# Fp32 value products in one query half of a clustered attention kernel with a maxout layer

## The chip, the cores and the metric

The kernel runs on one NeuronCore of one Trainium2 chip. Its engines are TensorE (PE in the rows, with PEld for its weight loads), VectorE (DVE), ScalarE (ACT), GpSimd (POOL) and SyncE (SP, which issues the DMAs). The metric is the device time of one execution in microseconds; 706.71 us is the median of three runs of the kernel before.

## The reference

```python
def _attn_ref(q, k, v, centroids):            # q, k, v: (4, 8, 768, 64)
    scale = 1.0 / np.sqrt(D)
    ...                                        # q_n, k_n, c_n: rows divided by their norm
    q_assign = np.argmax(np.einsum('bhsd,hcd->bhsc', q_n, c_n), axis=-1)    # 16 clusters
    k_assign = np.argmax(np.einsum('bhsd,hcd->bhsc', k_n, c_n), axis=-1)
    mask = q_assign[:, :, :, None] == k_assign[:, :, None, :]
    scores = scale * np.matmul(q, k.transpose(0, 1, 3, 2))
    scores = np.where(mask, scores, -1000000000.0)
    scores = scores - np.max(scores, axis=-1, keepdims=True)
    attn = np.exp(scores)
    attn = attn / (np.sum(attn, axis=-1, keepdims=True) + 1e-09)
    return np.matmul(attn, v).astype(np.float32)

def _moe_ref(x, w1, w2, w3, w_out):           # x: (3072, 512), w1..w3: (512, 768), w_out: (768, 512)
    h = np.maximum(np.maximum(x @ w1, x @ w2), x @ w3)
    return (h @ w_out).astype(np.float32)
```

All inputs and the output are fp32. The heads of the attention's output are joined to x.

## The kernel before

Most products are done in fp16 as sums of three: a tile is split into a high half (its fp16 value) and a low half (the rest, in fp16 again), and high x high, high x low and low x high are added in PSUM.

The attention goes by batch (4), query half (2, `gi`, three tiles of 128 queries each) and head pair (4): 32 visits (`visit`). A visit has 6 tiles (`tile_units`), one for each of two heads and three query tiles; a tile's number, counted over the whole program, is its `step` (0 to 191). One tile is 128 queries by 768 keys:

- `pe`: 4 matmuls make the scores in a PSUM tile `big` (L1252, L1254). Query and key carry mask rows.
- `mx`: VectorE scales them and takes the row minimum of their negative (L1263, and a small read of the accumulator).
- `exp`: ScalarE makes the exponentials and their row sums (L1269), into an SBUF tile `e` or in place in PSUM.
- Then the weights are turned, so that keys lie on the partitions, and split in two halves in the tile `pt`. Steps in `BY_PE` (even steps below 40): TensorE turns the fp32 tile with 6 transposes into another `big` (`ptr`, L1300), one copy makes the high half (`scaled`, L374 on ScalarE, L378 on VectorE) and VectorE subtracts for the low half (L1308). Other steps: the high half (L374, L376, L378) and the low half (L1275, in batches 1 to 3 also L1328) are made in SBUF in the tile `hl`, and one DMA transpose writes `pt` (L1278).

When a visit's 6 tiles are done, `av` adds 36 matmuls of 384 columns into one `big` (L1203). In batch 0 the row sums are spread over the partitions by 6 small fp32 products (`sums`, L1195), copied (`spread`) and multiplied in (`mult`, L1222), and the result is split in halves into `x16`. `ffn` then takes a half of a batch (384 tokens): 18 units of 12 matmuls (`hid`, L1409, weights `w16a` and `w16b`), whose maxima are taken by VectorE (L1423), and three units `outp` (L1464). It needs all four visits of its half.

Ahead of this the program prepares q and k per head pair (`prep`, with cluster products L778 and L787), v (`v_first` for batch 0, which loads v, takes its largest value with L917, scales and splits it; `v_prep` for the others), and the expert weights (`weights`). The tiles have fixed numbers of places (`caps`): 3 `big` in PSUM, 2 `e`, 4 `hl`, 4 `stage`.

The program is a list of units. `ORDER` gives the order in which they are written to the engines' queues, `HANDS` the engine (V, S, G, Q) of each unit that has a choice. Each engine works through its own queue in that order.

Of the kernel before, what the change touches and what calls it, by code (L numbers as in the profile page):

```python
# [27 lines left out]
0 3 1 4 2 5 7-14 6 16 15 18 19 51 52 173 151 30 54 21 17 20 22-27 39 401 53 153 28 55 31 33 36 40 56 41 57-59 32  # L28
60 61 42 35 63 64 29 67 34 37 65 66 174 43 73 44 74 45 86 154 152 85 88 87 89 90 68 69 46 97 155 38 47-50 156 62
# [4 lines left out]
1008 1009 986 987 1011 182-184 998 166 142 185 1010 972 445 1017 143 1012 988 186 1018 131 135 116 105 115 984  # L34
# [8 lines left out]
1138 1129 312 225 1115 226 1133 1134 313 1143 1135 1130 1139 1120 228 315 1144 1149 1150 1140 229-232 1116 316  # L43
# [5 lines left out]
2607 328 261 329 446 317 278-280 2608 1213 281 1196 265 1197 1214 1166 282 1198 283 417 1215 2609 262 435 330  # L49
# [13 lines left out]
473-475 2649 535 1343 1308 1317 1324 1295 1337 1344 1345 2652 1338 507 1339 501 503 1256 504 1297 476 1340 1296  # L63
# [19 lines left out]
631 1569 601 1602 605 1625 2729 606 1578 628 1633 1603 1626 2728 607 1627 1587 603 1612 1604 1570 2713 608 2733
1634 1628 2730 609 630 1642 2731 2732 1619 2735 632 633 1635 1636 2734 610 1650 611 1629 1643 1644 1620 2737
2736 1651 1637 673 1621 1645 612 1646 1630 1647 1652 1631 613 2738 1638-1640 2741 2742 1648 616 1667 1659 675
1668 1669 634 2743 635 1653 636 2739 604 2740 1660 2827 676 637 2767 1661 1649 1641 617 1679 677 638 640-642
2744 678 643 1622 1670 1654-1657 1662 1663 1680 1664 1665 644 1623 2745 1671 679-681 1624 1687 1681 682 1682
# [156 lines left out]
def kernel(  # L244
# [15 lines left out]
    P = 128  # L260
# [1270 lines left out]
```

## Time and profile before

| | us |
|---|---|
| three runs | 708.38, 706.71, 705.61 |
| median | 706.71 |
| profiled execution | 704.27 |
| its span, which the rows divide | 702.5 |
| TensorE busy | 661.4 (94%) |
| VectorE busy | 589.8 (84%) |
| ScalarE busy | 479.1 (68%) |
| GpSimd busy | 407.4 (58%) |

The span is what the profile sees between the first and the last instruction; 1.77 us of the execution lie around it. Shares of busy time are means over stretches that differ much, so the rows below cut the span. A busy TensorE is one with a matmul under way; the end of a group includes its last matmul's own time, so that groups which follow each other at once overlap a little.

### The profile page before, as it was taken

What the parts mean: (1) busy time and instruction counts of PE and PEld (TensorE: products, weight loads), DVE (VectorE), ACT (ScalarE), POOL (GpSimd) and SP (SyncE); (2) the same over time, 40 slices, a digit from 0 to 9 for tenths busy, and PEclk for the clock granted to TensorE, in tenths of its full rate; (3) what the DMA queues carried; (4) which work ended last, traced back from release to release, by engine and by line L of the source; (5) the groups of instructions that cost most, each with busy time, mean ns of one, the idle gap of its engine ahead of it and who ended that gap; (6) DMA issues with size and microseconds to landing.
All of it is one profiled execution on the core that took longest, in us unless ns stands there. A gap on an engine that the chain in (4) does not pass through costs nothing. (4 is left out here: it accounts for less than half of the span.)

```text
span 702.5 us, 13166 instructions
## 1 busy us (share of the span) xinstructions
PE 661.4 (94%) x4505; PEld 383.5 (55%) x4505; DVE 589.8 (84%) x1461; ACT 479.1 (68%) x840; POOL 407.4 (58%) x386
## 2 busy tenths in 40 slices
PE   3777879999999999999999999999999999999997
PEld 1555546655555555655555545565456646555563
DVE  7999999999998878989899788899899987883231
ACT  5899999999766557687866667796665666561001
POOL 3578886878647837876555626676577733431100
PEclk9999999999999999999999999999999999999999
DMA  7798888899979899999989897997998857866001
GB/s 256 206 170 193 218 215 209 209 181 197 175 187 187 159 183 196 200 176 207 202 170 201 166 188 170 196 194 167 221 216 162 168 114 152 151 133 139 16 1 45
DMA packets 297795, 121.03 MB, mean 172 GB/s; under 512 B 273024, under 2 KB 284160, under 8 KB 297728
## 3 DMA queue, kind: packets, MB, share of 16 engines
q1 hardware_dynamic: 297728, 120.20, 82.2%
q8 instruction: 35, 0.57, 0.3%
q14 instruction: 32, 0.26, 0.1%
HBM read 31.49 MB, written 6.29 MB: 54 GB/s over the span
## 5 line engine op out<-in xcount | busy, mean ns | idle before, releaser
L1263 DVE TENSOR_SCALAR_CACHE_REDUCE big<-big,nsc 128x768 f32<-128x768 f32 x192 | 193.6, 1017 | 14.8 <-PE big L1254 12.7
L1409 PE MATMUL one<-x,w16a 128*128 128x384 f16 x1152 | 197.6, 326 | 0.0
L1275 POOL TENSOR_TENSOR hl<-e,hl 128x768 f16<-128x768 f32 x88 | 146.7, 1670 | 60.4 <-ACT hl L374 27.0
L1409 PEld LDWEIGHTS <-w16a 128*128 128x128 f16 x1152 | 111.6, 98 | 75.6 <-issue 2.4
L1269 ACT ACTIVATE e<-big,nm 128x768 f32<-128x768 f32 x116 | 104.6, 902 | 60.4 <-DVE big L1263 23.7
L1252 PE MATMUL big<-qk 128*128 128x512 f16 (+1 forms) x384 | 96.3, 333 | 9.4 <-ACT e L1269 4.4
L1203 PE MATMUL big<-pt,v 128*64 128x384 f16 x1152 | 99.8, 327 | 1.8 <-DVE pt L1308 1.6
L1409 PE MATMUL one<-x,w16b 128*128 128x384 f16 x576 | 98.9, 326 | 1.2 <-DVE wf_h L378 0.7
L1254 PE MATMUL big<-qk 96*128 96x512 f16 (+1 forms) x384 | 96.2, 332 | 0.0
L1269 ACT ACTIVATE big<-big,nm 128x768 f32<-128x768 f32 x76 | 66.3, 872 | 27.6 <-DVE big L1263 22.5
L1203 PEld LDWEIGHTS <-v 128*64 128x64 f16 x1152 | 64.7, 110 | 35.0 <-issue 7.5
L1328 DVE SCALAR_TENSOR_TENSOR hl<-big,rs,hl 128x768 f16<-128x768 f32 x72 | 72.7, 1010 | 9.5 <-ACT hl L376 8.8
L1409 PEld LDWEIGHTS <-w16b 128*128 128x128 f16 x576 | 55.9, 98 | 39.2 <-issue 2.4
L376 ACT ACTIVATE hl<-big,rs 128x768 f16<-128x768 f32 x60 | 53.9, 898 | 23.5 <-issue 7.4
L378 POOL TENSOR_SCALAR hl<-e 128x768 f16<-128x768 f32 x40 | 34.3, 858 | 58.4 <-ACT e L1317 29.1
L1252 PEld LDWEIGHTS <-qk 128*128 128x128 f16 x384 | 34.8, 99 | 41.0 <-issue 16.4
L1254 PEld LDWEIGHTS <-qk 96*128 96x128 f16 x384 | 38.2, 99 | 26.5 <-issue 1.9
L814 POOL TENSOR_TENSOR qk<-stage,qk 128x768 f16<-128x768 f32 x27 | 45.3, 1679 | 8.2 <-ACT qk L374 7.6
L1464 PE MATMUL one<-wo,vf_h 128*128 128x512 f16 x216 | 48.5, 379 | 1.0 <-ACT wo L1129 1.0
L1464 PE MATMUL one<-wo,wf_h 128*128 128x512 f16 x216 | 48.3, 379 | 0.0
L1317 ACT ACTIVATE e<-e,rs 128x768 f32<-128x768 f32 x40 | 37.1, 931 | 7.5 <-DVE rs L1290 7.3
L1423 DVE SCALAR_TENSOR_TENSOR wf_h<-one,wf_h 128x384 f32<-128x384 f32 x48 | 26.5, 551 | 18.6 <-PE one L1409 18.2
(209 smaller groups left out, 1005.4 us busy)
## 6 DMA issues: line engine op xcount, KB each, us to landing
stage<-in_qk_dram SPq DMA_DIRECT2D x32, 384.0 KB, 4.2
wd<-in_moe_w_dram SPq DMA_DIRECT2D x18, 512.0 KB, 4.4
out_dram<-o SPq DMA_DIRECT2D x24, 256.0 KB, 2.5
qk<-qk SPq DMA_DIRECT2D x15, 384.0 KB, 4.5
qk<-qk SPq DMA_DIRECT2D x30, 192.0 KB, 3.3
stage<-in_v_dram SPq DMA_DIRECT2D x12, 384.0 KB, 4.2
wd<-in_moe_w_out_dram SPq DMA_DIRECT2D x6, 512.0 KB, 4.2
qk<-cl_t SPq DMA_DIRECT2D x60, 48.0 KB, 2.3
```

The costliest lines, as they stand in the source:

```text
L376: eng.activation(out, x, AF.Copy, scale=k)
L814: eng.tensor_tensor(t()[:, AQ, i], x(), t()[:, BQ, i], op=ALU.subtract)
L1203: nc.tensor.matmul(t()[D * i : D * i + D, 0:nb], v()[:, i, kt, a], pts[i % len(pts)]()[:, rows[i], c * QT + kt, :], start=(m == 0), stop=( ...
L1252: nc.tensor.matmul(t()[:, lo:hi], aq[:, qs], ak[:, lo:hi], start=True, stop=False)
L1254: nc.tensor.matmul(t()[:, lo:hi], bq[0:K2, qs], bk[0:K2, lo:hi], start=False, stop=True)
L1263: nc.vector.tensor_scalar(s, s, -SCALE if exact else nscs[:, b, pr : pr + 1], 3.0e38, op0=ALU.mult, op1=ALU.min, accum_out=nm())
L1269: nc.scalar.activation(e(), t()[:, 0:S], AF.Exp, bias=nm(), scale=-1.0, accum_out=r)
L1275: eng.tensor_tensor(hl()[:, 1, :], e(), hl()[:, 0, :], op=ALU.subtract)
L1317: eng.activation(e(), e(), AF.Copy, scale=r())
L1328: eng.scalar_tensor_tensor(hl()[:, 1, :], e(), r(), hl()[:, 0, :], op0=ALU.mult, op1=ALU.subtract)
L1409: nc.tensor.matmul(t()[:, 0:nb], w16[jt // JA][:, jt % JA, wa, i, ct], x16[b, gi, ct]()[:, xa, 0:nb], start=(m == 0), stop=(m == 3 * CT - 1),)
L1464: nc.tensor.matmul(t()[:, 0:DM], h16(jt)[:, ha, tt * P : (tt + 1) * P], wo16[0][:, jt, wa, :], start=(m == 0), stop=(m == 3 * JT - 1),)
```

## The change

In the first query half of batch 0 (`gi` in `V32`, 4 visits, steps 0 to 23) all tiles go by TensorE's transposes, are copied out of PSUM once, in fp32, and are not split. The value product takes these and v itself in fp32: 12 products instead of 36. The factor that v was scaled by is put into the spread row sums. For the second half of batch 0 v is loaded again, head pair by head pair, then scaled and split. `e` and `hl` become one kind of place, 6 of them. `ORDER` and `HANDS` are new throughout.

```diff
@@ ORDER @@
-0 3 1 4 2 5 7-14 6 16 15 18 19 51 52 173 151 30 54 21 17 20 22-27 39 401 53 153 28 55 31 33 36 40 56 41 57-59 32
+0 1 3 4 2 5-14 18 20 15 16 19 21-23 30 24 17 52 51 54 39 53 177 25 40 26 153 151 55 27 56 28 41 31 33 36 35 57
...
+    V32 = {0}
...
-        "big": 3, "one": 2, "stage": 4, "e": 2, "hl": 4, "pt": 3, "rs": 3, "v16": 4, "qk": 4,
+        "big": 3, "one": 2, "stage": 4, "e": 6, "pt": 3, "rs": 3, "v16": 4, "qk": 4,
...
@@ v_first @@
+        u_vs[0], vinv[0] = u, s
         for pr in range(NPAIR):
-            prio = start[0, pr] + V_LEAD
-            def sc(eng, pr=pr):
-                y = x[pr // 2]()[:, (pr & 1) * S : (pr & 1) * S + S]
...
+            v32[pr], u_v32[pr] = x[pr // 2], u_ld[pr // 2]
+            y = pool_lease(sb, "stage", [P, S], F32)
+            prio = start[0, pr] + 24 + V_LEAD
+
+            def again(pr=pr, y=y):
+                nc.sync.dma_start(out=y(), in_=vv[0, :, 2 * pr : 2 * pr + 2].rearrange("p h t d -> p (h t d)"))
...
@@ visit @@
+        f32 = not b and gi in V32
...
+        def av32():
+            for kt in range(QT):
+                for i in range(2):
+                    x = pts[i % len(pts)]().rearrange("p g c q -> p (g c q)").bitcast(F32)
+                    x = x.rearrange("p (g c q) -> p g c q", g=G, q=P)
+                    vx = v()[:, (pr & 1) * S : (pr & 1) * S + S].rearrange("p (h t d) -> p h t d", h=2, d=D)
+                    nc.tensor.matmul(
+                        t()[D * i : D * i + D, 0:nb],
+                        vx[:, i, kt],
+                        x[:, rows[i], kt, :],
+                        start=(kt == 0),
+                        stop=(kt == QT - 1),
+                    )
...
-            scaled(eng, xr(), ts()[:, 0:nb])
+            scaled(eng, xr(), ts()[:, 0:nb], vinv[b]() if f32 else 1.0)
...
@@ tile_units @@
-        pool = by_pool(step) or step in BY_PE or step in BY_16
+        pool = by_pool(step) or step in BY_PE or step in BY_16 or f32
...
-        hl = None if step in BY_PE else pool_lease(sb, "hl", [P, 2, S], F16)
+        hl = None if step in BY_PE or f32 else pool_lease(sb, "e", [P, S], F32)
...
-        if step in BY_PE:
+        if step in BY_PE or f32:
...
             u = add("PE", 1.3, ptr, [u], [ex, o], step)
+            if f32:
+
+                def take32(eng):
+                    d = pt()[:, at].rearrange("p c q -> p (c q)").bitcast(F32)
+                    scaled(eng, d, o()[:, 0:S])
+
+                u_t.append(add({"ACT": 0.69, "DVE": 0.86}, 0, take32, [u], [o, pt], step))
+                return
```

What the new order moves is seen at three places. First VectorE near the start. `vmax<-vf` are the two reductions of v (L917, now L929), `cl_t_210<-onehot_99` (now `cl_t_201<-onehot_99`) is the transposition of the first head pair's cluster rows, which the first score tile needs. Before:

```order
L611 TENSOR_SCALAR onehot_99<-cl_t_210,ksel 128x768
L917 TENSOR_REDUCE vmax<-vf 128x1 x2
L735 TENSOR_SCALAR q_m<-q_m_268 128x1
L739 TENSOR_SCALAR q_m<-q_m 128x1
L622 STREAM_TRANSPOSE cl_t_210<-onehot_99 128x768
L401 TENSOR_REDUCE sc_m<-vmax 128x1
```

and now:

```order
L610 TENSOR_SCALAR onehot_99<-cl_t_201,ksel 128x768
L767 TENSOR_REDUCE q_s<-q_r 128x1
L572 STREAM_TRANSPOSE cl_t_256<-big 128x768
L929 TENSOR_REDUCE vmax<-vf 128x1
L581 TENSOR_REDUCE cl_m<-cl_t_256 128x24
L621 STREAM_TRANSPOSE cl_t_201<-onehot_99 128x768
L929 TENSOR_REDUCE vmax<-vf 128x1
```

One of the two reductions now stands behind that transposition.

Then VectorE around the first visit's row sums (L1188, now L1207). `big,nm<-big,nsc` is the row minimum `mx`, `pt<-big,pt` the low half of a tile turned by TensorE, `wf` and `wmx` belong to the expert weights. Before:

```order
L1263 TENSOR_SCALAR big,nm<-big,nsc 128x768
L1308 TENSOR_TENSOR pt<-big,pt 128x768
L758 TENSOR_REDUCE q_s<-q_r 128x1
L1263 TENSOR_SCALAR big,nm<-big,nsc 128x768
L1188 RECIPROCAL rs<-rs 128x6
L1066 TENSOR_REDUCE wmx<-wf 128x1
L395 TENSOR_SCALAR sc_m<-wmx 128x1
L392 TENSOR_SCALAR sc_m<-sc_m 128x1
L1308 TENSOR_TENSOR pt<-big,pt 128x768 x2
```

and now, around the first visit's last step on VectorE (L1255, before L1222) and the second visit's row sums:

```order
L1043 SCALAR_TENSOR_TENSOR wf<-wd,top 128x512
L1299 TENSOR_SCALAR big,nm<-big,nsc 128x768
L533 TENSOR_REDUCE cl_m_445<-cl_t_444 128x24
L1299 TENSOR_SCALAR big,nm<-big,nsc 128x768
L538 TENSOR_TENSOR cl_t_444<-rank,cl_m_445 128x768
L411 RECIPROCAL sc_s<-vp_116 128x1
L1043 SCALAR_TENSOR_TENSOR wf<-wd,top 128x512
L1255 TENSOR_TENSOR xs<-big,xs 128x384
L391 TENSOR_SCALAR sc_m<-sc_m 128x1
L1299 TENSOR_SCALAR big,nm<-big,nsc 128x768 x2
L1207 RECIPROCAL rs<-rs 128x6
```

Between two row minima there is no low half any more; small pieces of the preparation stand there.

Last TensorE ahead of the first value product. `big<-ident,e` are transposes (6 for a tile), `one<-ident,rs` the spread row sums, `big<-qk` scores. Before:

```order
L1300 MATMUL big<-ident,e 128x128 x12
L1195 MATMUL one<-ident,rs 64x128 x6
L1252 LDWEIGHTS qk
L1252 MATMUL big<-qk 128x512
L1252 LDWEIGHTS qk
```

and now:

```order
L1290 MATMUL big<-qk 128x256
L1214 MATMUL one<-ident,rs 64x128 x6
L1336 MATMUL big<-ident,e 128x128 x12
L407 LDWEIGHTS sc_m
L407 MATMUL one<-ident,sc_m 128x128
L1336 MATMUL big<-ident,e 128x128 x12
```

Four tiles are turned at the end of the first visit, where two were.

## Rows read from the trace of the kernel before

**Rows 1.** The page: engines' busy us, share of the span, instructions.

```profile
PE 661.4 (94%) x4505; PEld 383.5 (55%) x4505; DVE 589.8 (84%) x1461; ACT 479.1 (68%) x840; POOL 407.4 (58%) x386
```

**Rows 2.** Stretches: length, busy of PE, PEld, DVE, ACT, POOL, clock, DMA share, GB/s.

```profile
26.35:105.26 78.91, 61.72 (x455) 38.81 (x456) 77.44 (x156) 74.43 (x135) 63.17 (x52) 0.98 0.88 203
105.26:180.00 74.74, 72.67 (x526) 43.77 (x524) 72.75 (x192) 73.21 (x133) 58.76 (x52) 1.00 0.91 200
180.00:651.00 471.00, 467.47 (x3214) 267.06 (x3213) 406.23 (x1034) 309.40 (x540) 272.68 (x239) 1.00 0.90 176
651.00:702.50 51.50, 47.55 (x274) 26.57 (x272) 12.22 (x24) 4.26 (x7) 2.85 (x4) 0.99 0.06 21
```

**Rows 3.** Timeline of TensorE to 45 us: start, duration, what, [idle before].

```profile
13.23 2.83 PE L778 MATMUL big<-stage,cwf 128*64 128x512 f32 x8
20.52 5.30 PE L787 MATMUL one<-cwn,stage 128*128 128x32 f32 x24 [4.46 <-DMA stage<-in_qk_dram]
...
26.35 0.85 PE L1252 MATMUL big<-qk 128*128 128x512 f16 x2
...
42.80 0.29 PE L745 MATMUL one<-ident,q_m 128*128 128x128 bf16 x1 [1.14 <-DVE cl_t L551]
42.90 0.83 PE L1252 MATMUL big<-qk 128*128 128x512 f16 x2
...
44.17 0.85 PE L1252 MATMUL big<-qk 128*128 128x512 f16 x2
```

**Rows 4.** Timeline of TensorE from 78 to 106 us.

```profile
78.38 0.88 PE L1195 MATMUL one<-ident,rs 128*64 128x128 f32 x12
...
81.45 0.48 PE L1252 MATMUL big<-qk 128*128 128x512 f16 x2
81.78 0.49 PE L1254 MATMUL big<-qk 96*128 96x512 f16 x2
...
98.70 3.12 PE L1203 MATMUL big<-pt,v 128*64 128x384 f16 x36
...
101.82 0.82 PE L1300 MATMUL big<-ident,e 128*128 128x128 f32 x6
102.48 0.49 PE L1252 MATMUL big<-qk 128*128 128x512 f16 x2
...
105.26 2.11 PE L1409 MATMUL one<-x,w16a 128*128 128x384 f16 x12
```

**Rows 5.** TensorE's waits, 26.35 to 105.26 us: for whom, us, times, longest.

```profile
PE big L1252 <- ACT e L1269: 4.2, 6, 1.5
PE big L1300 <- ACT e L1269: 4.2, 5, 1.2
PE big L1252 <- DVE pt L1308: 2.9, 5, 0.9
PE big L1203 <- DVE pt L1308: 1.6, 2, 1.1
```

**Rows 6.** VectorE's groups up to 109 us: busy us, mean ns, idle before.

```profile
L1308 DVE TENSOR_TENSOR pt<-big,pt 128x768 f16<-128x768 f32 x15 | 14.2, 950 | 0.1
...
L378 DVE TENSOR_SCALAR hl<-e 128x768 f16<-128x768 f32 x2 | 1.1, 544 | 0.0
```

**Rows 7.** ScalarE's groups up to 105.26 us.

```profile
L1269 ACT ACTIVATE e<-big,nm 128x768 f32<-128x768 f32 x30 | 27.1, 905 | 2.1 <-DVE big L1263 1.7 <-POOL hl L1275 0.2
L374 ACT CAST pt<-big 128x768 f16<-128x768 f32 x14 | 11.1, 800 | 1.0 <-PE big L1300 0.9
L374 ACT CAST hl<-e 128x768 f16<-128x768 f32 x12 | 10.1, 838 | 0.1
```

**Rows 8.** GpSimd's largest group up to 105.26 us.

```profile
L1275 POOL TENSOR_TENSOR hl<-e,hl 128x768 f16<-128x768 f32 x13 | 22.7, 1745 | 6.9 <-ACT hl L374 2.9 <-DVE q_r L757 2.1 <-DVE hl L378 1.7
```

**Rows 9.** TensorE's groups by form, 45.5 to 105.26 us.

```profile
L1195 PE MATMUL one<-ident,rs 128*64 128x128 f32 x48 | 3.5, 281 | 0.0
```

**Rows 10.** Busy time as in rows 2, from 42.00 to 45.50 us.

```profile
42.00:45.50 3.50, 2.70 (x10) 1.41 (x11) 3.36 (x9) 2.49 (x6) 2.67 (x2) 0.60 1.18 130
```

More of the change, by code (lines that the diff above doesn't have):

```diff
@@ L83 @@
[L83 to L87, printed above, removed]
[3 rows of a table removed]
@@ new lines @@
+749 750 2777 2781 1814 1831 751 2778 1846 752 1847 1823 1815 2782 1824-1826 2783 2785 1841 1827 1842 2779 1816
+2780 1848 676 1849 1863 2784 1832 1850 1833 2786 1864 1855 2789 2787 1865 1856 753 1817 1818 2791 1851-1853 1843
+1866 2753 1828 2790 1857 1858 1844 756 754 743 755 1845 1834 1867 1835-1837 1819 1859 1860 2926 1861 1883 1875
+2793 815 1862 2788 2927 2792 1884 1820 1868 1869 1900 2794-2796 1870 1854 1871 1885 1892 1901 1902 1893 1894
+2797 1876 1877 1909 1903 1886 1895 1896 1887 2798 1897 1888 1878-1880 1904 1910 765 766 1898 1881 2799 1911-1913
@@ new lines @@
+1905 1914 1889 2865 2801 2800 1917 1915 2802-2804 1890 1918 1872 1882 1899 1937 2808 1938 1919-1921 1873 1906
+1939 1929 1940 1922 1941 1874 1954 1946 2811 1891 1916 1923 1924 1947 1955 1948 1956 1949 1950 1930 1951 2809
+1952 1957 1931 1907 1908 1942-1944 1925 1932 1963 1964 1958 1965 1959 1966-1968 1933 1934 1969 2814 1926 2750
+2810 770 1953 1970 1945 2812 1927 1935 1960 1961 1928 2866 1983 1971 1991 1972 1984 2815 773 1973 1974 2867 1992
+2817 2000 2819 1985-1987 1936 2813 2818 1993-1996 1975 1976 772 1988 2008 2001 2002 1977 1978 2820 2009 1997
@@ new lines @@
+1998 2816 1962 861 2821 2822 774 1979 1989 2010 2011 2003 2825 2826 2823 2012 775 2013 2017 776-778 2004 2005
+779 780 785 2824 2025-2027 2018 2827 786 2829 2006 2028 2828 782 2019 2020 2830 2029 1990 783 781 2021 787 2045
+1999 2007 2022 2046 2047 2831 784 1980 816 2023 788 2037 818 817 2030 2014 2031 2032 792 2038 2039 1981 2048
+1982 2040 793 2015 2041 794 860 2833 2834 2042 2054 2062-2064 789 2832 819 820 2055 790 2024 2835 2049 2837 795
+2056 2836 2065 2043 2033 2016 821 2071 2050 2051 2079 2057 796 2838 2052 2839 797 2080 822-824 862 825 827 2841
@@ new lines @@
+2193 2202-2204 2886 2222 2888 2194 854 923 855 856 2205 2241 2889 2233 2213 941 2242 2214 894 893 2893 857 2195
+2223 2206 2890 927 2243 2891 2894 942 2227 2234 2892 2235 899 2253 2895 2254 2228 928 2255 2256 2244 2257 2258
+2196 924 2215 925 2229 2230 900 2236 2231 2896 2897 929 943 2237 2245 2259 2238 858 930 2239 931 932 2260 901
+933 2232 2240 926 2261-2263 2270 2901 934 2271 2264 2898 935 2278 2272 2899 2273 2902 2900 2903 2274 2279
+2246-2248 2904 938 2275 2280 2276 2905 939 2876 944-946 950 951 2265 2281 2266 2267 916 2295 2282 2287 2296 2297
@@ new lines @@
+2965 2963 2533 2534 2507 2535 2536 2493 2959 2960 2523 2524 2537 2964 2466 2966 2467 2468 2969 2970 2540
+2482-2484 2967 2502 2968 2485 2971 2541 2516 2508 2525 2542 2509 2510 2517 2973 2972 2974 2548 2538 2526 2527
+2549 2977 2979 2550 2565 2543 2528 2544 2545 2539 2978 2551 2546 2975 2976 2552 3045 2518 2557 2566 2529 2558
+2519 2981 2520 2559 2553 2554 2980 2982 2560 2547 2561 2983 2555 2530 2984 2562 2567 2563 2568-2571 2994 2991
+2572 2556 2564 2573 2992 2574-2576 2521 2522 3046 2995 2993 2988 2989 2997-3002 3005-3007 3009 3003 3004 3008
@@ L168 @@
+VSGSVVVVSVVGGSVVSGVVVGGSVVSGVSSSVVGGSVVSGVVVGGSVVSGSVVGGVVVVVSSSSVVSGSVVSGSVVSGSVVGGSVVVGSVVGGSVSSVVGGVVVSGSVVGG
+VVVSVSVVGGSVVSVVSVSVVGVSVVGGVVVGVSVVGGVVVGVSVVVVSSVSVVSGVVVVVSVVSGSVVVVSVVGGVVVVVSVS
 """
@@ L625, in mask_rows @@
             u = first_rows(base, fast, cl, u_cl, ct, cols, bc)
+        elif exact:
+            u = add("DVE", 0.89, tr1, [u_cl], [cl, ct], base)
+            u = add("DVE", 0.47, red, [u], [ct], base)
+            u = add({"DVE": 0.47} if fast else {"POOL": 0.8, "DVE": 0.47}, 0, sub, [u], [ct], base, port=True)
+            u = plan.chain("DVE", [(0.47, pick, 1), (0.46, red2), (0.47, hot, 1)], [u], [ct], base)
+            u = add({"DVE": 0.33}, 0, hot4, [u], [ct, oh4], base, port=True)
+            u = add("DVE", 0.89, tr4, [u], [ct, oh4], base)
+            rows = raw_rows(base, fast, ct, u, t)
+            u_raw.extend(rows)
+            return rows
         else:
@@ L889 @@
     vrel = {}
+    u_vs, vinv = {}, {}
     v16 = {}
@@ L903, in v_tail @@
         u_v[b, pr] = add({"POOL": 1.6, "DVE": 0.85}, 0, lo, [u], extra + [v], in_prio, port=True)
+    v32, u_v32 = {}, {}
     def v_first():
@@ L919, in mx, with sc @@
                 )
-            u = add("SP", 0.6, load, (), [x[i]], V_LOAD, work=3.1)
-            us.append(add("DVE", 1.67, mx, [u], [x[i]], V_MAX))
+            u_ld.append(add("SP", 0.6, load, (), [x[i]], V_LOAD, work=3.1))
+            us.append(add("DVE", 1.67, mx, [u_ld[i]], [x[i]], V_MAX))
         u, s = pow2_units(vmax[:, 0, 0:2], vp0, V_MAX, us, True)
         vsc[0] = vp0
+        u_vs[0], vinv[0] = u, s
         for pr in range(NPAIR):
-            prio = start[0, pr] + V_LEAD
-            def sc(eng, pr=pr):
-                y = x[pr // 2]()[:, (pr & 1) * S : (pr & 1) * S + S]
+            v32[pr], u_v32[pr] = x[pr // 2], u_ld[pr // 2]
[3 more added lines that the diff above has]
+                nc.sync.dma_start(out=y(), in_=vv[0, :, 2 * pr : 2 * pr + 2].rearrange("p h t d -> p (h t d)"))
+            def sc(eng, y=y):
                 if eng is nc.scalar:
-                    eng.activation(y, y, AF.Copy, scale=s())
+                    eng.activation(y(), y(), AF.Copy, scale=s())
                 else:
-                    eng.tensor_scalar(y, y, s(), 1.0, op0=ALU.mult, op1=ALU.mult)
-            k = add({"ACT": 0.84, "POOL": 0.95, "DVE": 0.46}, 0, sc, [u], [x[pr // 2], s], prio, port=True)
-            part = lambda pr=pr: x[pr // 2]()[:, (pr & 1) * S : (pr & 1) * S + S]
-            v_tail(0, pr, part, k, prio, [x[pr // 2]])
+                    eng.tensor_scalar(y(), y(), s(), 1.0, op0=ALU.mult, op1=ALU.mult)
+            k = add("SP", 0.6, again, (), [y], prio - 3, work=1.6)
+            k = add({"ACT": 0.84, "POOL": 0.87, "DVE": 0.53}, 0, sc, [k, u], [y, s], prio, port=True)
+            v_tail(0, pr, y, k, prio, [y])
     def v_prep(b, pr):
@@ L1164, in visit @@
         k = gn / G
-        v = v16[b, pr]
+        v = v32[pr] if f32 else v16[b, pr]
+        u_vl = u_v32[pr] if f32 else u_v[b, pr]
         if norm:
@@ L1226, in visit @@
         u_s = add("PE", 0.27 * gn, sums, [u], [rs, ts], p)
-        u_c = add({"ACT": 0.08 + 0.3 * k, "DVE": 0.07 + 0.4 * k}, 0, spread, [u_s], [ts, xs], p)
-        u = add("PE", av_cost(gn), av, u_t + [u_v[b, pr]], pts + [v, t], p)
+        u_c = add({"ACT": 0.08 + 0.3 * k, "DVE": 0.07 + 0.4 * k}, 0, spread, [u_s] + ([u_vs[b]] if f32 else []), [ts, xs] + ([vinv[b]] if f32 else []), p)
+        u = add("PE", 4.0 * gn / 3 if f32 else av_cost(gn), av32 if f32 else av, u_t + [u_vl], pts + [v, t], p)
         u = add("DVE", 0.1 + 0.4 * k, mult, [u, u_c, u_vc.get(b)], [t, xs], p)
@@ L1271, in hi @@
         def hi(eng):
-            scaled(eng, hl()[:, 0, :], e())
+            scaled(eng, hv()[:, 0, :], e())
         def lo(eng):
-            eng.tensor_tensor(hl()[:, 1, :], e(), hl()[:, 0, :], op=ALU.subtract)
+            eng.tensor_tensor(hv()[:, 1, :], e(), hv()[:, 0, :], op=ALU.subtract)
         def tr():
-            nc.sync.dma_start_transpose(out=pt()[:, at], in_=hl().rearrange("p a s -> p (a s)"))
+            nc.sync.dma_start_transpose(out=pt()[:, at], in_=hv().rearrange("p a s -> p (a s)"))
         exact = (b, pr) in RAW
```

113 lines of the change are left out of this document (48 added, 65 removed), and 139 rows, old and new, of the table ORDER.

## The prediction

> **What bounds the kernel now.** I began with the page. TensorE is busy for 661.4 of 702.5 us [rows 1], so nearly all of the span is its own work, and a change that adds work to it has to buy that back from its idle time. Where that idle time lies, the table of busy time by stretches tells [rows 2]. I cut it at 26.35 us, where the first score tile starts [rows 3], and at 105.26 us, where the first matmul of the expert layer starts [rows 4].
>
> - From 26.35 to 105.26 (78.91 us) VectorE is busy for 77.44, ScalarE for 74.43 and TensorE for 61.72. TensorE idles for 17.2 us here, VectorE for 1.5: the two others feed TensorE, and they set this stretch.
> - From 105.26 on TensorE has the expert layer's matmuls to fill its gaps. It idles 2.1 us up to 180, 3.5 us in the next 471, and 4.0 in the last 51.5. This part is TensorE's own work, and nothing else moves it.
>
> Third come TensorE's waits between the two cuts [rows 5]. It waits 8.4 us for exponentials (their result, or the PSUM place that they free), and 4.5 us for L1308, the subtraction that makes the low half of a weight tile turned by TensorE. The rest, 4.3 us, stands behind small chains. So the time is the moment at which the expert layer can start (call it T, 105.26 now), plus 597.24 us in which TensorE is full. The change touches only the first query half of batch 0, all of whose work lies ahead of T. I therefore forecast T, and keep the 597.24.
>
> **The change, part by part.** The first query half of batch 0 has 4 visits of 6 tiles, 24 tiles. Before, 12 (even steps) are turned by TensorE and split out of PSUM, and 12 (odd steps) are split in SBUF and turned by a DMA transpose.
>
> *Removed.* The 12 even tiles lose L1308 on VectorE: 12 x 0.950 = 11.4 us [rows 6]. The 12 odd ones lose the high half (in the program's order 9 on ScalarE at 0.838, 2 on VectorE at 0.544, 1 on GpSimd), the low half (11 on GpSimd at 1.745, one on VectorE, for which I take the same 0.95) and the transpose's issue [rows 6 to 8]. The 12 first copies of the even tiles (11 on ScalarE at 0.800, 1 on VectorE, again 0.95) go as well.
>
> *Added there.* 24 copies from PSUM to SBUF in fp32, by the order 20 on ScalarE and 4 on VectorE. The trace has none that writes fp32 over 768 columns; the nearest rows are the same copy to fp16 (0.800) and the exponential, which reads PSUM and writes fp32 (0.905) [rows 7]. I take 0.87, between them, and 0.95 for VectorE's 4.
>
> *Sum on the feeders.* VectorE: -11.4 - 1.1 - 0.95 - 0.95 + 3.8 = -10.6 us. ScalarE: -7.5 - 8.8 + 17.4 = +1.1. GpSimd: -19.2 for the low halves. GpSimd's free time is used: counted in the order up to the first expert matmul, ScalarE does 17 scalings and casts of q, k, v, x and the weights fewer and 4 other pieces more, and GpSimd takes most of them, or they come later (batch 0's value split). These net 13 run over half to all of the 768 columns for which a cast needs 0.838: 5.4 to 10.9 us, most of them wide; I take 9. With the 1.1 ScalarE is then 8 us shorter up to that point.
>
> *Added on TensorE.* 12 more tiles of 6 transposes. A group of 6 shows 0.82, but the next group starts 0.66 after it began (101.82 to 102.48) [rows 4]; I take 0.72, between them: 12 x 0.72 = 8.6 us. The value product goes from 36 fp16 matmuls to 12 products in fp32, of two instructions each. The trace has none of these with 384 columns, so I bound it. From above: L778, fp32 with 64 weight columns, took 2.83 us for 8 instructions, four of 512 and four of 256 columns, 3072 in all [rows 3], so 0.92 ns a column; 24 x 384 columns are then 8.5 us. From below: the fp16 product takes 3.12 us for 36 matmuls [rows 4], some 0.1 of it the last one's overhang, so 0.084 each, and 24 are 2.0 us. Between lies L1195, also fp32 with 64 weight columns and two heads side by side: 12 instructions of 128 columns in 0.88 [rows 4], each 0.28 long [rows 9], so (0.88 - 0.28) / 11 = 0.055 from start to start, and three times that for 384 columns: 24 x 0.165 = 3.97 us. L778 lies ahead of 26.35 and L1195 in the stretch itself, so I take 3.97 against 3.02, four times: +3.8 us (bounds -4 and +22). By the order one more score tile (0.65, twice the spacing of its two halves, 81.45 to 81.78 [rows 4]) stands ahead of the first expert matmul; it is missing behind it.
>
> *The start.* The first score tile needs cluster rows that VectorE makes; a reduction of v that stood ahead of them now stands behind. But on TensorE that tile follows 24 cluster matmuls which waited 4.46 us for a load and ran to 25.82 [rows 3]. So 0.5 us is won if the load comes as before; I take 0.5, bounds 0 and 4.5.
>
> *Sharing places.* Exponentials had 2 places and split tiles 4; now 6 serve both, and in this half nothing is split, so an exponential finds a place sooner. I cost this at nothing, a gain at most. The v tiles are loaded a second time, 4 loads of 384 KB, on the queue that 12 transposes have left; I cost that at nothing too.
>
> **The sum.** TensorE's busy time in the stretch becomes 61.7 + 8.6 + 3.8 + 0.65 = 74.8. Where waits go, groups close up: a score tile alone shows 0.82 (81.45 to 82.27), one followed at once 0.65. Of the 18 waits in the four groups of rows 5 and the few small ones I count 15 gone, at 0.16 each, 2.4 us: 72.4. The stretch is then 72.4 plus the idle time that is left, which I call L, from a start at 25.8. The span changes by 25.8 + 72.4 + L - 105.26 - 0.65 = L - 7.7 us. All hangs on L, 17.2 now. The 4.5 us behind L1308 go with it. The others were waits for feeders that ran full; their work to T shrinks by 10.6 and 8 us while TensorE's grows by 13, so against TensorE's need they are some 20 us ahead, more than all its waits. But then VectorE (66.8 of 76), ScalarE (66) and TensorE (72) are all near nine tenths full, each in a fixed order, with three large PSUM places between them, so some waits stay. I take a third of the 12.7 that L1308 doesn't cause: L = 4.0. That puts T at 102.2, the span at 698.8 and the profiled execution at 704.27 - 3.7 = 700.6. The profiled execution lies 2.4 under the median of the runs, 706.71; from that, 703.0 us.
>
> **A rule against it.** From 42.00 to 45.50 us the granted clock was 0.60 on average [rows 10], between the two levels of 1.2 and 2.4 GHz, and a score tile took 1.27 there (42.90 to 44.17) [rows 3] for 0.65 elsewhere; just before, TensorE had idled 1.14. In the stretch as a whole, all of the first half's transposes included, it was 0.98 [rows 2]. The Trainium skill (TensorE: Matmul & The Clock Gate, Part 4: PE-mode transpose) says that transposes don't count as activity for the clock in the way that other matmuls do; by that rule twice as many of them would hold it up less, and rival 4 would be likelier. No fall behind a group of transposes stands out in this trace.
>
> **Rivals.**
> 1. *The feeders are so far ahead that L is about 0.* T is then 98.2 and the change -7.7: 699.0 us. For it: VectorE alone would allow 94.7, ScalarE 97.3. Against it: no stretch without expert matmuls shows TensorE full. Chance 0.20.
> 2. *Slower: the waits are round trips, not late feeders.* Each tile goes scores, maximum, exponential, transposes, copy, and holds a large PSUM place twice, now all 24 tiles and not 12; with three places TensorE may wait as often as before. L stays at 17.2 and nothing closes up: 25.8 + 74.8 + 17.2 - 105.26 - 0.65 = +11.9, 718.6 us. For it: 4.2 us are waits for places that exponentials free. Against it: L1308 held such a place too, and goes. It decides from L = 7.7 on; slower by over 0.5% needs L over 11.2. Chance 0.12. Half of it, L between 7 and 11, gives 706 to 710: chance 0.12.
> 3. *The fp32 product runs at L778's pace*: 4 x 4.5 = +18 us on TensorE, 721. Against it: L1195. Chance 0.04.
> 4. *The clock falls more often between 26 and 105.* Three score tiles cost 0.62 us more each from 42.0 to 45.5; two more such falls are 3.7 us, 706.7. Against it: the new order leaves TensorE less idle. Chance 0.06.
> 5. *The change doesn't move T*: the expert layer waits for its converted weights, whose chain is as long as before. 706.1. Against it: 15 weight loads stand ahead of that point in the old order, 16 in the new. Chance 0.06.
>
> The forecast has 0.40, its own range 700 to 706.
>
> **How the numbers follow.** What a measurement can tell from no change is about 0.5%, 3.5 us: under 703.2 is faster, over 710.2 slower. Faster: rival 1 and a little over half of the forecast, 0.42. Slower: rivals 2 and 3 and a hundredth of the rest, 0.17. Within: 0.41. The range reaches to rival 1 with a margin below, and into rival 2 above: 697 to 711; outside lie the far side of 2, and 3.
>
> **What the profile after would show.** First expert matmul near 102 (right), at or over 105 (wrong). TensorE's idle time between its first score tile and that point near 4 instead of 17; no wait for a low half in the first query half. A value product of 24 instructions in about 4.0 us; a group of transposes still at 0.82. VectorE under 95% in that stretch. From the first expert matmul to the end still about 597. The prediction is wrong if TensorE waits over 8 us for the new copies or for exponentials there, or idles behind T where it doesn't now.

## The result, and the profile after

The changed kernel took 695.47 us (median of 4, 694.62 to 696.72), the kernel before 706.16 beside it (4 runs, 703.82 to 708.38): ratio 0.985, 95% interval 0.981 to 0.989. Two repeats gave 0.988 (0.984 to 0.992) and 0.987 (0.985 to 0.989). The change makes the kernel 1.2 to 1.5% faster. The forecast was 703.0, its range from 697: the sign was right, the gain two to three times as large as forecast. The profiled execution took 696.72 us, 7.55 less than the one of before.

The page's row of busy time, to set against [rows 1]:

```profile
PE 669.1 (96%) x4529; PEld 389.3 (56%) x4529; DVE 584.4 (84%) x1452; ACT 463.1 (67%) x814; POOL 408.8 (59%) x394
```

The table of stretches, cut where the first score tile starts (23.74) and where the first expert matmul starts (99.97); columns as in [rows 2]:

```profile
23.74:99.97 76.23, 71.34 (x483) 44.78 (x484) 70.44 (x150) 67.16 (x126) 51.60 (x49) 0.94 0.59 170
99.97:180.00 80.03, 78.21 (x576) 47.13 (x575) 78.58 (x197) 76.67 (x136) 63.83 (x55) 1.00 0.86 195
180.00:643.40 463.40, 461.09 (x3161) 263.87 (x3156) 404.20 (x1033) 296.43 (x521) 281.01 (x247) 1.00 0.92 178
643.40:694.90 51.50, 47.63 (x275) 26.59 (x272) 11.48 (x23) 5.05 (x9) 3.25 (x4) 1.00 0.07 26
```

TensorE does 9.6 us more work in the first stretch than in [rows 2], and the stretch is 2.7 us shorter: its idle time there fell from 17.2 to 4.9 us. VectorE fell from 98% to 92% of the stretch, TensorE rose from 78% to 94%. The DMA engines' share fell from 0.88 to 0.59. The stretch also starts 2.6 us earlier, so the first expert matmul moved by 5.3, and what follows it takes 594.93 us in place of 597.24.

TensorE's waits in that stretch, to set against [rows 5] (for whom, us, times, longest), and below them the longest of ScalarE and VectorE:

```profile
PE one L754 <- DVE q_m L748: 1.7, 1, 1.7
PE big L1288 <- ACT e L1305: 1.7, 3, 0.7
PE big L1288 <- ACT pt L373: 0.5, 2, 0.2
PE big L1288 <- DVE pt L1352: 0.4, 1, 0.4
...
ACT pt L373 <- PE big L1336: 5.4, 6, 2.1
ACT e L1305 <- DVE big L1299: 2.4, 4, 1.6
DVE big L1299 <- PE big L1290: 1.9, 6, 0.7
```

The wait for low halves is gone from the first query half (the 0.4 us is one in the second). Now ScalarE waits for TensorE's transposes. The direction of waiting has turned round.

TensorE's timeline at the end of the stretch, to set against [rows 4]:

```profile
89.87 0.87 PE L1336 MATMUL big<-ident,e 128*128 128x128 f32 x6 [0.15 <-ACT e L1305]
90.81 4.09 PE L1225 MATMUL big<-pt,vf 128*64 128x384 f32 x24
94.83 0.23 PE L407 MATMUL one<-ident,sc_m 128*128 128x128 bf16 x1
94.90 0.82 PE L1336 MATMUL big<-ident,e 128*128 128x128 f32 x6
97.41 0.23 PE L754 MATMUL one<-ident,q_m 128*128 128x128 bf16 x1 [1.68 <-DVE q_m L748]
```

The fp32 value product takes 4.02 us to the next start (90.81 to 94.83); 3.97 were forecast. The start, TensorE's timeline, to set against [rows 3]:

```profile
16.63 0.61 PE L796 MATMUL one<-cwn,stage 128*128 128x32 f32 x2 [3.16 <-DMA stage<-in_qk_dram]
19.02 4.90 PE L796 MATMUL one<-cwn,stage 128*128 128x32 f32 x22 [1.79 <-DMA stage<-in_qk_dram]
23.74 0.83 PE L1288 MATMUL big<-qk 128*128 128x512 f16 x2
```

The load for these cluster matmuls is issued behind VectorE's low half of the first head pair. In the trace of before, VectorE's and then SyncE's row of it:

```profile
13.80 1.00 DVE L800 SCALAR_TENSOR_TENSOR qk<-stage,q_s,qk 128x768 f16<-128x768 f32 x1
```

```profile
14.88 2.82 SPq L721 DMA_DIRECT2D stage<-in_qk_dram  x2
```

and after:

```profile
12.52 1.01 DVE L809 SCALAR_TENSOR_TENSOR qk<-stage,q_s,qk 128x768 f16<-128x768 f32 x1
```

```profile
13.61 1.72 SPq L730 DMA_DIRECT2D stage<-in_qk_dram  x2
```

VectorE reaches this low half 1.28 us earlier, the load goes out 1.27 earlier, most of the cluster matmuls start at 19.02 in place of 20.52, and the first score tile follows them directly at 23.74.

The two feeders' groups in the stretch (busy us, mean ns of one, idle before), VectorE's to set against [rows 6], ScalarE's against [rows 7]:

```profile
L1299 DVE TENSOR_SCALAR_CACHE_REDUCE big<-big,nsc 128x768 f32<-128x768 f32 x31 | 31.2, 1020 | 2.4 <-PE big L1290 1.9 <-ACT pt L373 0.3
L1043 DVE SCALAR_TENSOR_TENSOR wf<-wd,top 128x512 int32<-128x512 int32 x13 | 10.4, 801 | 0.2 <-DVE w16a L1059 0.2
...
L377 DVE TENSOR_SCALAR pt<-big 128x768 f32<-128x768 f32 x4 | 3.8, 948 | 0.0
```

```profile
L1305 ACT ACTIVATE e<-big,nm 128x768 f32<-128x768 f32 x30 | 27.1, 907 | 2.5 <-DVE big L1299 2.4
L373 ACT COPY pt<-big 128x768 f32<-128x768 f32 x20 | 15.6, 807 | 5.5 <-PE big L1336 5.4
```

The copies out of PSUM are 20 and 4, as counted, at 0.807 us (0.87 taken) and 0.948 (0.95).

### The profile page after: what moved, and what is told of

Read it like the earlier page. It is cut to its first block, busy times and chain, and to the rows that moved or that the text cites. A ratio compares the mean times of both kernels' runs of the same rounds, so it can differ in the third digit from the quotient of the medians.

```text
span 694.9 us, 13112 instructions
## 1 busy us (share of the span) xinstructions
PE 669.1 (96%) x4529; PEld 389.3 (56%) x4529; DVE 584.4 (84%) x1452; ACT 463.1 (67%) x814; POOL 408.8 (59%) x394
## 5 line engine op out<-in xcount | busy, mean ns | idle before, releaser
L1311 POOL TENSOR_TENSOR e<-e 128x768 f16<-128x768 f32 x77 | 127.2, 1654 | 42.2 <-ACT e L373 31.2
L1236 PE MATMUL big<-pt,v 128*64 128x384 f16 x1008 | 87.3, 327 | 0.0
L1372 DVE SCALAR_TENSOR_TENSOR e<-big,rs,e 128x768 f16<-128x768 f32 x72 | 72.5, 1011 | 5.4 <-ACT e L375 4.9
L1236 PEld LDWEIGHTS <-v 128*64 128x64 f16 x1008 | 55.8, 110 | 29.2 <-issue 6.8
L375 ACT ACTIVATE e<-big,rs 128x768 f16<-128x768 f32 x55 | 49.4, 899 | 28.6 <-DVE rs L1326 11.6
L377 POOL TENSOR_SCALAR e<-e 128x768 f16<-128x768 f32 x38 | 31.6, 833 | 37.6 <-ACT e L1361 15.4
L823 POOL TENSOR_TENSOR qk<-stage,qk 128x768 f16<-128x768 f32 x29 | 47.7, 1651 | 8.1 <-ACT qk L373 7.3
L1363 POOL TENSOR_SCALAR e<-e,rs 128x768 f32<-128x768 f32 x31 | 28.4, 917 | 37.1 <-DVE rs L1326 23.7
```

The costliest lines, as they stand in the source:

```text
L375: eng.activation(out, x, AF.Copy, scale=k)
L377: eng.tensor_scalar(out, x, k, 1.0, op0=ALU.mult, op1=ALU.mult)
L823: eng.tensor_tensor(t()[:, AQ, i], x(), t()[:, BQ, i], op=ALU.subtract)
L1236: nc.tensor.matmul(t()[D * i : D * i + D, 0:nb], v()[:, i, kt, a], pts[i % len(pts)]()[:, rows[i], c * QT + kt, :], start=(m == 0), stop=( ...
L1311: eng.tensor_tensor(hv()[:, 1, :], e(), hv()[:, 0, :], op=ALU.subtract)
L1372: eng.scalar_tensor_tensor(hv()[:, 1, :], e(), r(), hv()[:, 0, :], op0=ALU.mult, op1=ALU.subtract)
```

## The experiments

Theory A is the forecast's: VectorE and ScalarE set the first stretch before; relieved, they leave it to TensorE. Its rivals: the earlier start alone; round trips that the order makes; lighter DMA traffic. Theories B and C, in the expectations below, are forms of A: in B what counts is where in the order an operation waits, in C that both feeders had to be relieved. The new `ORDER` was never run without the fp32 product, nor the fp32 product in the old order, so what the order gives alone is not known. Where a kernel did not run beside the changed one, I set its ratio against 0.987, the middle of the three above; 0.1% is 0.7 us, and such a difference is good to some 2 to 3 us.

### One subtraction more, with its wait, and the same work without it

```diff
                     scaled(eng, d, o()[:, 0:S])
+                    if not step % 2:
+                        nc.vector.tensor_tensor(o()[:, 0:S], o()[:, 0:S], d, op=ALU.subtract)
```

> The changed kernel with one more VectorE operation behind the PSUM copy of each even tile of the first query half: a subtraction in the same PSUM tile, 12 of about 0.95 us, the cost and the place of the L1308 that the change took away (the transposed weights are unchanged). Theory A (VectorE and ScalarE set the stretch before, and freeing VectorE moved the first expert matmul): VectorE is busy for 67.2 of 76.2 us now, 9.1 free, so 11.4 more bring it over; the first expert matmul comes 2.3 to 6 us later, and the run is 2 to 6 us longer. Rival (the gain is the earlier start, the fuller rest and less DMA traffic, and L1308 was off the path): 0 to 1 us.

718.32 us, 22.0 over the changed kernel beside it (ratio 1.020 to before, 1.014 to 1.026): far over either expectation. The stretch, VectorE's largest wait and TensorE's for the same operation, and two rows of VectorE's timeline:

```profile
23.19:121.44 98.25, 77.92 (x484) 48.16 (x484) 79.38 (x164) 69.08 (x126) 51.06 (x49) 0.91 0.46 133
```

```profile
DVE big L1348 <- ACT pt L373: 11.2, 8, 2.5
PE big L1225 <- DVE big L1348: 5.1, 2, 4.1
```

```profile
30.16 0.15 DVE L400 TENSOR_REDUCE sc_m<-vmax 128x1 f32<-128x2 f32 x1
32.79 0.97 DVE L1348 TENSOR_TENSOR big<-big,pt 128x768 f32<-128x768 f32 x1 [2.48 <-ACT pt L373]
```

VectorE is busy for 79.4 of 98.3 us: it is not full. It stands still behind ScalarE's copy, and the maxima queued behind it come late. The subtraction also holds its PSUM place for longer, and TensorE waits for that. So this run does not price L1308's work; it prices a wait and a held place, which it does not tell apart. The next has nearly the same work (12 operations of 0.945 us, the subtractions took 0.969) without either:

```diff
+                    if not step % 2:
+                        nc.vector.tensor_reduce(junk[:, 0:6], <ident, six times>, axis=AX.X, op=ALU.max)
```

> The changed kernel with 12 more VectorE operations of about 0.95 us, where the experiment that put a subtraction back had its 12, but with nothing to wait for and nobody waiting (a maximum over the constant unit matrix into a scratch column). It has the same VectorE work as that experiment (+22 us against the changed kernel) without its round trip. Theory A in its plain form (VectorE's and ScalarE's work sets the stretch; what counts is busy time): about as long as with the subtraction, 12 us or more. Theory B (what counts is the order: VectorE stood still behind ScalarE's copy, and its later maxima with it; bare work mostly finds the 9 us that are free): 1 to 6 us.

701.35 us, ratio 0.993 (0.990 to 0.996): 4.2 over the changed kernel, as theory B expects. Theory A falls in the form in which all busy time counts (12 us or more): the 12 operations lengthened VectorE's busy time by 8.7 us and cost half of that, and behind a wait five times as much.

```profile
24.00:104.64 80.64, 72.32 (x483) 44.27 (x484) 79.17 (x162) 67.99 (x126) 51.06 (x49) 1.00 0.55 160
```

The free time was smaller than both expectations say: in the changed kernel VectorE is busy for 70.44 us of 76.23, so 5.8 us were free; the 67.2 of the first expectation is ScalarE's figure. With the 8.7 us more VectorE is busy for 98% of the stretch, as in the kernel before, and the stretch is 1.5 us longer than its busy time, as there. So a full VectorE sets this stretch again, which is theory A in the form of a limit.

### ScalarE's work given back

Four small activations behind each even tile's copy:

```diff
+                    for _ in range(0 if step % 2 else 4):
+                        nc.scalar.activation(junk, ident[:, 0:8], AF.Copy)
```

> The changed kernel with 48 more small ScalarE operations (four behind each even tile's copy, 0.2 us each by the row of the smallest activations: 9.6 us), with nothing to wait for. ScalarE is busy for 67 of 76 us now. If ScalarE's relief (8 us by the forecast) is a part of the gain: 2 to 8 us longer. If only VectorE's counted: 0 to 1.5 us.

702.11 us, ratio 0.995 (0.993 to 0.998): 5.8 over the changed kernel, for 7.8 us more ScalarE work:

```profile
23.74:105.89 82.15, 72.56 (x484) 44.83 (x485) 70.78 (x150) 74.99 (x174) 51.29 (x49) 0.94 0.55 159
```

ScalarE is not full here (75.0 of 82.2 us), so a limit does not explain this cost; how it comes about was not traced. And the reassignment itself, eight pieces put back on ScalarE by number:

```diff
+        for n in (102, 99, 135, 98, 134, 198, 192, 216):
+            self.units[n].hand = nc.scalar
```

> The changed kernel with eight casts and scalings that the new order gave to GpSimd back on ScalarE (three high halves of q and k, two scalings, three of x; 3 x 0.84 + 2 x 0.94 + 3 x 0.72 = 6.6 us). Theory C (both feeders had to be relieved: the reassignment to GpSimd, which the low halves had kept busy, is as large a part of the gain as L1308): 3 to 5 us longer than the changed kernel, since 8 us of bare ScalarE work cost 5. If the reassignment only follows and gains nothing: under 1.5 us.

701.19 us, ratio 0.992 (0.990 to 0.995): 3.7 over the changed kernel, as theory C expects. The casts that GpSimd took are part of the gain.

### TensorE's work doubled

```diff
-            for kt in range(QT):
+            for kt in [*range(QT), *range(QT)]:
```

> The changed kernel with the fp32 value product of the first query half done twice, 4 x 4.1 us more on TensorE and nothing more on any other engine. If TensorE is the bound of the stretch now (71.3 of 76.2 us busy): 13 to 16.5 us longer. If the feeders still set the stretch and TensorE only follows, the 4.9 us of idle time hide that much at most, and the waits for exponentials shrink with it: 9 to 12 us. If the gain hangs on the clock that a fuller TensorE is granted: less than 9.

711.23 us, 14.9 over the changed kernel beside it.

```profile
23.93:113.70 89.77, 84.96 (x580) 49.71 (x581) 70.23 (x150) 67.87 (x127) 51.27 (x49) 0.98 0.49 144
```

TensorE's busy time grew by 13.6 us and the stretch by 13.5. Its idle time stayed at 4.8: nothing of the added work was hidden. TensorE bounds the stretch now.

### Each relief alone, in the kernel before

```diff
-                "DVE", 0.86, lambda: nc.vector.tensor_tensor(part(1), o()[:, 0:S], part(0), op=ALU.subtract), ...
+                "DVE", 0.86, lambda: nc.vector.memset(part(1), 0.0) if step < 24 else nc.vector.tensor_tensor(...), ...
```

> The kernel before, with the 12 subtractions L1308 of the first query half replaced by writing zeros (0.3 us or so each; the low half of these weights is left out of the result). If L1308's work and wait on VectorE were the main cost that the change took away: 4 to 8 us faster than the kernel before, the first expert matmul that much earlier. If the gain came from the rest (start, sources of the odd tiles, DMA): 0 to 2 us.

703.20 us against 705.87: ratio 0.997 (0.994 to 1.001), no gain that can be told from none. The stretch and TensorE's waits, to set against [rows 2, 5]:

```profile
26.34:106.95 80.61, 63.31 (x454) 39.25 (x455) 72.24 (x156) 74.05 (x135) 63.74 (x52) 0.89 0.90 202
```

```profile
PE big L1252 <- ACT e L1269: 7.1, 9, 1.5
PE big L1300 <- ACT e L1269: 6.9, 6, 1.5
```

VectorE has 5.2 us less to do, and the 4.5 us that TensorE waited for low halves are gone, but its waits for exponentials rose from 8.4 to 14.0. The wait was replaced by the next one in line.

```diff
+        for n in (102, 99, 135, 98, 134, 191, 194, 215):
+            self.units[n].hand = nc.gpsimd
```

> The kernel before with the same eight casts and scalings moved from ScalarE to GpSimd (6.6 us off ScalarE; GpSimd goes from 63 of 79 us to 70), nothing else. Theory C: little alone, 0 to 2 us faster, since VectorE (77.4 of 78.9) still sets the stretch, or slower, where GpSimd's casts come late behind its low halves. If ScalarE alone set the stretch: 4 to 6 us faster.

> The kernel before with both: zeros in place of the 12 subtractions L1308 of the first half (their low halves are left out of the result) and the eight casts and scalings on GpSimd. Theory C: the two together give clearly more than the sum of each alone, 4 to 7 us faster than the kernel before. If each feeder counts by itself: the sum of the two, about 2 to 3 us. If TensorE's waits are round trips that no relief shortens: under 2 us.

The second run has both edits. Both are slower: 711.76 us (ratio 1.008, 1.005 to 1.011) and 711.94 (1.010, 1.006 to 1.014). So theory C's gain from the two together does not come in this form. In the kernel before GpSimd makes the odd tiles' low halves; casts put among them make these late, and they hold the places that the next exponentials need. The moved kernel's and then the combined kernel's wait, which was 0.2 us before:

```profile
ACT e L1271 <- POOL hl L1277: 6.9, 4, 2.9
```

```profile
ACT e L1271 <- POOL hl L1277: 8.9, 5, 2.6
```

In the old order GpSimd could not take ScalarE's casts without loss; in the new it could, with the low halves of this half off it.

### The start

> The changed kernel with one entry of the order put back: the second reduction of v on VectorE stands ahead of the cluster rows of the first head pair again (3.4 us of VectorE). Theory A with TensorE as the bound of the stretch: a first score tile that is late by d makes the whole run late by nearly d, 2 to 3.4 us. Rival (the feeders set the stretch, so what is lost at the start is made up before the first expert matmul): 0 to 0.7 us.

```diff
+        order.remove(152)
+        order.insert(order.index(46), 152)
```

696.96 us, 0.6 over the changed kernel. It tested the wrong entry: its first score tile starts at 23.33, so the reduction of v was not what had held the start. VectorE's rows ahead of the first low half point to another entry. Before, it idled 1.45 us ahead of four small copies and took the first maximum of the first head pair (`q_m`) behind them:

```profile
6.45 0.22 DVE L498 COPY cwf<-one 64x64 f32<-64x64 f32 x1 [1.45 <-ACT cw L484]
7.20 0.95 DVE L729 TENSOR_REDUCE q_m<-stage 128x1 f32<-128x768 f32 x1
```

In the changed kernel it takes that maximum ahead of the copies:

```profile
4.63 0.94 DVE L738 TENSOR_REDUCE q_m<-stage 128x1 f32<-128x768 f32 x1
```

That entry was not put back. The next run delays the first low half itself:

```diff
             def lo_s(i=i, x=x):
+                for _ in range(3 if (b, pr, i) == (0, 0, 0) else 0):
+                    nc.vector.tensor_reduce(junk[:, 0:6], <ident, six times>, axis=AX.X, op=ALU.max)
```

> The changed kernel with three VectorE operations of 0.95 us (a maximum over the constant unit matrix) ahead of the first low half of the first head pair, so that everything behind them at the start, the load that TensorE waits for among it, comes about 2.6 us later, as in the kernel before. If the start passes through to the end: 2 to 3 us longer than the changed kernel. If the stretch makes it up: under 1 us.

699.40 us, ratio 0.992 (0.989 to 0.994): 3.2 over the changed kernel. The first score tile came at 25.93, 2.2 later, and in the profiled execution the first expert matmul 1.6 later (101.57). A late start passes through.

### The transfers

24 writes of 256 KB in the first half, from the exponentials, then from a constant with no wait, then only 12 of those:

```diff
+                    if step % 2:
+                        for m in range(2):
+                            r = step // 2 * 2 * P + m * P
+                            nc.sync.dma_start(out=out[r : r + P, :], in_=ex()[:, 256 * m : 256 * m + 512])
```

> The changed kernel with 24 writes of 256 KB more in the first query half (two behind each odd tile, to rows of the output that are written over later), which give the DMA engines back traffic of the kind that went with the 12 transposes (DMA share of the stretch 0.88 before, 0.59 now). If lighter traffic is a part of the gain (loads of weights, q, k and v landing sooner): 1 to 4 us longer. If not: under 1 us.

> The changed kernel with the same 24 writes of 256 KB, from the constant unit matrix (in rows of 512 bytes) instead of the exponentials: the same bytes at the same places of the queue, but none of them waits for a tile or holds an exponential's place. If the traffic itself costs (loads land later): as long as with the writes of exponentials, 6 to 9 us over the changed kernel. If it was the queue's waits and the held places: 0 to 3 us over it.

> The changed kernel with 12 of the 24 extra writes from the constant matrix, one behind each odd tile. If the cost of 24 (6 us by the ratios) follows the bytes: 2 to 4 us longer than the changed kernel beside it. If there is a threshold (loads are late only when the queues are full): under 1 us.

705.54 us (ratio 1.000, 0.997 to 1.003), 704.84 (0.997, 0.993 to 1.000) and 698.66 (0.991, 0.989 to 0.993): 9.0, 6.8 and, beside the changed kernel (695.37), 3.3 over it. In these sizes the cost follows the bytes. The 2.2 us between the first two are within the noise, so a cost of queueing and held places is not shown. The second kernel's stretch and its longest wait, which is 3.4 us in the changed kernel:

```profile
23.36:110.42 87.06, 72.96 (x483) 44.48 (x484) 73.06 (x151) 67.81 (x126) 51.86 (x49) 0.96 0.79 223
```

```profile
POOL top L1039 <- DMA wd<-in_moe_w_dram: 9.8, 2, 5.3
```

Weights for the expert layer land later, GpSimd and ScalarE wait for them in their fixed order, and the tiles' work behind them is late. In the profiled execution of the third kernel, the fastest of its six, T did not move (99.68), so how 12 writes cost is not shown. The bytes are like those that went, not the same: with the transposes the stretch lost packets under 512 bytes, 19,904 before and 2,224 now. How much they cost in the order of before was not tried; its weight loads took a median of 4.3 us to land in the stretch, the changed kernel's 4.0, and 5.3 with the second kernel's writes.

### Tries for a faster kernel

Five more pieces from ScalarE to GpSimd:

> The changed kernel with five more pieces moved from ScalarE to GpSimd in the first stretch (three casts of weights, two halves of x; about 3.6 us off ScalarE; GpSimd is busy for 52 of 76 us). If ScalarE's bare work still counts with about 0.6 of its size (8 us given back cost 5): 1 to 2.2 us faster. If the moved pieces come late on GpSimd, as in the old order: 1 to 5 us slower.

698.14 us, ratio 0.987 (0.983 to 0.990): no change. Filler matmuls at the start, in the form that leaves every product as it is:

> The changed kernel with 15 filler matmuls of 512 columns at the start, four ahead of a pair's maxima and eleven ahead of the first cluster matmul of the third head pair, in PSUM places that are written over before they are read. If the low clock behind the start costs: 1 to 4 us faster than the changed kernel beside it. If the feeders hide it: within 0.7 us.

697.22 us against 695.37 for the changed kernel beside it (ratios 0.989 and 0.987, their intervals overlap): no gain. The fillers did not do what they were for. The first score tile still ran at the pace of the low clock (0.83 us for its first two matmuls, 0.48 later on), so whether that clock costs anything stays open. The repeats give a hint, from single executions: in one the score pairs reached the fast pace at 28 us instead of 33, and its stretch took 75.65 us against 76.23 and 76.32. An earlier form had four of the fillers between the first cluster matmuls of the third head pair:

> The changed kernel with 15 fp16 matmuls of 512 columns on TensorE while it waits at the start (four ahead of a pair's maxima, eleven ahead of and among the cluster matmuls of the third head pair), written over before anyone reads them. In the profiled execution of the changed kernel the granted clock was 0.50 from 23.74 to 33.00 us, and TensorE was busy for 8.69 of these 9.26. If that clock costs: 1 to 4 us faster. If the feeders hide it there: within 0.7 us.

They were not written over in time there: some cluster products of that pair are lost in its result. It took 695.58 us, ratio 0.983 (0.979 to 0.986), with the first score tile at 22.34 us and again at 0.83 for its first two matmuls. The changed kernel did not run beside it, and the form that keeps all products shows no gain, so I draw nothing from it.

## Why the prediction was wrong

**The mechanism was right.** The feeders set the stretch; relieved, they leave TensorE 94% full; T moved to 99.97 (102.2 forecast), the idle time L is 4.9 (4.0 forecast), the fp32 product follows L1195's pace. Rival 1 (L near 0), rival 2 (L stays at 17.2) and rival 3 (L778's pace) are out; so is rival 5, since T moved. Rival 4 has nothing behind it: the granted clock reads 1.00 from 33 us to T, and no score pair from 34 us on took over 0.5 us.

**The sizes were off, four of them towards a shorter time.** In the forecast's own sum, on the profiled executions:

| term | forecast | measured | difference |
|---|---|---|---|
| start | 25.8 | 23.74 | -2.1 |
| TensorE busy in the stretch | 72.4 | 71.34 | -1.1 |
| L | 4.0 | 4.89 | +0.9 |
| from T to the end | 596.6 | 594.93 | -1.7 |
| sum (span) | 698.8 | 694.9 | -3.9 |
| to the median of the runs | +4.2 | +0.6 | -3.6 |

1. *The start.* The step "0.5 us is won if the load comes as before" failed: the load did not come as before. Its issue waits for a low half on VectorE that the new order reaches 1.28 us earlier. The order shows that; I looked at one reduction that moved and not at what the load waits for. The held start shows that such time is not made up later.
2. *The median.* The forecast added 2.4 us because the one profiled execution of before lay that far under a median of three runs. Over 11 to 31 runs beside the later experiments the medians of before are 703.97 to 705.87, and the profiled execution (704.27) lies among them. After the change it lay 1.25 above its median. The 2.4 was scatter, and together with the other side it makes nearly half of the miss.
3. *The rest.* "Nothing else moves it" was too strong: from T on, TensorE idles 8.0 us instead of 9.6, and 0.8 us of work went. In the two repeats this part took 593.65 and 593.37 us. The cause was not tested.
4. *The busy time* closed up 1.1 us more than counted. The two traces hold a candidate, which no run tests. Before, TensorE also ran at the slow pace from 42.90 to 45.45 us: two tiles (the forecast says three), whose four pairs start 0.64 us apart and not 0.33, 1.2 us more in all. After the change there is no such spell, but one more group of transposes stands in the slow start (1.48 us for 0.87).

**One step was wrong though its number came out.** "The 4.5 us behind L1308 go with it": alone they don't. With L1308's work gone in the old order, waits for exponentials took their place. L fell when VectorE, ScalarE, GpSimd's low halves and the transfers were relieved together, in a new order; the parts were not separated. In the changed kernel 8.7 us of VectorE's work cost 4.2 back, 7.8 of ScalarE's 5.8, 2.2 us of start 3.2, 24 writes 6.8; 13.6 on TensorE cost 14.9. These overlap and are no shares of the gain, but they show why 9.6 us more on TensorE could be bought back and more.

**One term was not in the sum at all.** The transposes left SyncE's queue, and the forecast costed what that gives at nothing (it only asked whether the second load of v is hidden). The extra writes show that the stretch of the changed kernel feels the DMA engines' load. And VectorE's relief was smaller than forecast: 70.4 us busy, not 66.8; 1.4 of that is 13 conversions of weights that took 0.80 us each in place of 0.69. That L still came out near 4.0 is then partly luck: less relief on VectorE, and perhaps more from the transfers, which the sum left out.

## What to carry to other kernels

Where three engines feed a fourth in a fixed order, the time behind one named wait is not what removing that wait gives: look for what is late next, and relieve all that are near full, the transfer queues too. For the start, follow the first transfer that the bound engine waits for back to the instruction that releases its issue, and see where the new order puts that one. Take no offset between one profiled execution and a median of three; that alone made a third of this forecast's miss.

## What was unexpected of the hardware

The clock column can mislead over a stretch. In the kernel with the moved reduction it reads 1.00 from 23.33 to 33.00 us, but its first matmuls took as long as those of the changed kernel, where it reads 0.50:

```profile
23.33:33.00 9.67, 7.91 (x32) 4.80 (x33) 7.76 (x21) 8.33 (x16) 2.52 (x2) 1.00 0.66 199
```

```profile
23.33 0.83 PE L1290 MATMUL big<-qk 128*128 128x512 f16 x2
```

```profile
23.74:33.00 9.26, 8.69 (x37) 5.69 (x38) 8.39 (x21) 7.60 (x16) 3.18 (x3) 0.50 0.69 200
33.00:46.60 13.60, 13.54 (x109) 10.36 (x107) 12.29 (x31) 13.19 (x25) 8.45 (x8) 1.00 0.69 198
```

The third fence is the changed kernel's; 0.50 is the lower of the two levels, 1.2 GHz. The same pair of matmuls takes 0.48 us from 34 us on. The kernel before has the same:

```profile
26.00:30.00 4.00, 3.74 (x13) 1.87 (x14) 4.00 (x11) 3.68 (x6) 1.97 (x3) 1.00 0.98 304
```

```profile
29.65 0.85 PE L1254 MATMUL big<-qk 96*128 96x512 f16 x2
```

All its score pairs up to 34 us took 0.83 to 0.85 us. So the forecast's 0.98 for the whole stretch, and its 0.65 for a score tile "elsewhere", left out a slow spell at the start. Here the length of a known instruction tells the clock better than that column.

With all 24 tiles turned by TensorE the granted clock from 33.00 to 46.60 us reads 1.00 (last row of the changed kernel above), and the score tiles there run at the fast pace, 0.48 us for their pairs. The rule of the Trainium skill that the forecast weighed (TensorE: Matmul & The Clock Gate, Part 4: PE-mode transpose) does not show in these rows. They do not refute it: the transposes stand between score tiles and value products here, so no run shows what they do alone.
